# Decode attention over a long key/value cache: loads with 24 KB rows, fewer places, another order and cut of the last loads, and the even head turned at once

## The chip, the cores and the metric

One core of a Trainium2 chip runs the whole program; nothing else runs beside it. The metric is device time in microseconds (us) of one execution, as the median of several. The median of the kernel before moves by 0.3 us between rounds (2007.43 to 2007.76).

## The reference

```python
# x: 1x1x640;  k_cache, v_cache: 32 heads x 32768 keys x 192, bf16;  wq: 640x6144;  wo: 6144x640
h  = x + attention(layernorm(x), k_cache, v_cache, wq, wo)     # one query, softmax over 32768 keys a head
h2 = h + relu(layernorm(h) @ w1) @ w2                          # w1: 640x1536, w2: 1536x640
```

One token attends over a cache of 2 x 403 MB. Nearly all the bytes are read once and used in a few operations, so moving them is the first suspect for the bound; the profile below agrees (DMA queue 98.3%, busiest compute engine 74%).

## The kernel before

Keys and values come in loads of 32 keys per partition: 128 partitions x 12,288 bytes, 1.5 MB, in five places (buffers) for keys and five for values. Of each 32 keys, TensorE turns (transposes) and multiplies 20 (`jp`), VectorE multiplies and sums 12. The product with V follows one chunk later.

```python
J = 32
for h in range(H):
    parts = [(J, 20)] * NC                       # (keys per partition, of these on TensorE)
    if h == H - 1:
        parts = [(J, 20)] * (NC - 1) + [(16, 10), (8, 4), (8, 4)]
...
kpool = ctx.enter_context(tc.tile_pool(name="kpool", bufs=5))
vpool = ctx.enter_context(tc.tile_pool(name="vpool", bufs=5))
...
def load_kv(g):
    h, c, k0, jc, jp = chunks[g]
    kt = kpool.tile([P, J * Dh], bf16, tag="kt", name="kt")
    nc.sync.dma_start(out=kt[:, 0:jc * Dh],
                      in_=k_hd[h, k0:k0 + P * jc, :].rearrange("(p j) d -> p (j d)", p=P))
    vt = ...                                     # the same for values
...
def load_w(name, src, pool, tag, c0, c1):        # w1 and w2 in half loads, each on 128 partitions
    ...
    nc.sync.dma_start(out=v, in_=src.rearrange("(c p) n -> p c n", p=P)[:, c0:c1, :])
...
def o_turn(pr):                                  # two heads' outputs (192 each) into three columns of 128
    ...                                          # ten f32 products with selection matrices
    nc.scalar.copy(out=oT[:], in_=ps[:])
...
for g in range(G):
    if g == G - 3:
        load_w("w1", ...); load_w("w1", ...); load_w("w2", ...); load_w("w2", ...)
    if g > 0:
        load_kv(g)
    transposes(g)
    if g > 0:
        pv(g - 1)
    scores_pe(g)
    sc = scores_dve(g)
    ...
```

The softmax here doesn't subtract the row's maximum and nothing guards it: scores larger than these inputs give would overflow.

## Time and profile before

| | before |
|---|---|
| time, median (range) | 2007.57 us (2007.49 to 2007.66), three runs |
| span in the profile | 2005.7 us |
| busiest compute engine | PE, 74% |
| DMA queue of the loads | 98.3% of the 16 DMA engines' time |
| rate, mean over the span | 413 GB/s |
| rate in undisturbed stretches | 419 to 425 GB/s |

How to read it: a share of the span near 100% names a suspect, and the chain that ended last tells whether the time hangs on it. Here both say DMA (98.3% of the engines' time, 93% of the chain). The 40 slices of the DMA rate then show where it is less than full, and the finer stretches show why. In a stretch, a packet counts where it starts, so a share can come out a little over 1. The lines are in the prediction and are not repeated, but for the rate in 40 slices, which is not there:

```profile
GB/s 396 423 422 422 423 422 423 420 423 424 421 424 417 423 423 422 424 405 424 423 422 423 395 425 422 423 424 396 423 422 424 423 401 424 422 424 422 423 418 171
```

Two things used throughout are in the trace but not in the printed views: the record of every DMA packet (size, start, duration) and the landing records (one count per DMA engine and load). "Step" below is the time from one packet's start to the next packet's start on the same DMA engine. The **trailing half** are eight DMA engines that count in later (16.5 to 18.7 us after a load's first count near 860 us); that they are the ones that also fetch the program's instructions is inferred from the sizes of the gap and of the fetches. The **leading half** are the other eight. Which physical DMA engines these are, the records do not say; the halves are told apart by the gap between their counts.

### The profile page before, as it was taken

How to read it: one execution, taken by the hardware profiler on the slowest of the kernel's cores; microseconds unless marked ns; L12 is line 12 of the kernel's file. 1: busy time of each engine (PE TensorE's matmuls, PEld its weight loads, DVE VectorE, ACT ScalarE, POOL GpSimd, SP SyncE). 2: the span in 40 equal slices, each digit the busy share in tenths (PEclk: the TensorE clock that was granted, in tenths of full speed). 3: DMA queues.
4: the chain of work that ended last, by engine and by line, in shares of the span. 5: the costliest groups of instructions: out<-in, count | busy, mean ns of one | idle time of the engine just before them, and what ended most of it. 6: DMA issues, size and time to landing. Idle time of an engine off the chain costs nothing.

```text
span 2005.7 us, 62124 instructions
## 1 busy us (share of the span) xinstructions
PE 1485.8 (74%) x28712; PEld 1452.7 (72%) x28712; DVE 1333.4 (66%) x646; ACT 1066.1 (53%) x2206; POOL 0.7 (0%) x6
## 2 busy tenths in 40 slices
PE   5777787867778778776777777877777777777775
PEld 5776686767777668676777776877777777777775
DVE  5766676667676667666766676666676667666664
ACT  4555555555555555555555455554555545555553
POOL 0000000000000000000000000000000000000000
PEclk7665656566665666666565665565565755665656
DMA  9999999999999999999999999999999999999994
GB/s 396 423 422 422 423 422 423 420 423 424 421 424 417 423 423 422 424 405 424 423 422 423 395 425 422 423 424 396 423 422 424 423 401 424 422 424 422 423 418 171
DMA packets 88472, 828.97 MB, mean 413 GB/s; under 512 B 8724, under 2 KB 21524, under 8 KB 22932
## 3 DMA queue, kind: packets, MB, share of 16 engines
q1 hardware_dynamic: 88212, 825.00, 98.3%
q8 instruction: 224, 3.67, 0.7%
q14 instruction: 36, 0.29, 0.0%
HBM read 824.97 MB, written 0.00 MB: 411 GB/s over the span
## 4 chain that ended last, share of the span: by engine, by line
DMA 93%; PE 5%; DVE 1%; SPq 1%; issue 0%; ACT 0%; DVEq 0%; ACTq 0%
DMA kt<-in_A_k_cache_dram 78%; DMA vt<-in_A_v_cache_dram 15%; PE tp L230 3%; DVE pr L257 1%; PE oT_ps L320 1%; PE o_ps L288 0%; SPq L113 0%; PE o_ps L290 0%; PE o_ps L286 0%; DVE sc L260 0%; PE sp L240 0%; SPq L110 0%; PE sp L244 0%; PE sp L242 0%; PE yps L391 0%
## 5 line engine op out<-in xcount | busy, mean ns | idle before, releaser
L231 ACT COPY kT<-tp 128x1024 bf16<-128x1024 bf16 (+1 forms) x1024 | 908.0, 974 | 670.0 <-PE tp L230 670.0
L230 PE MATMUL tp<-ident_b,kt 128*128 128x128 bf16 x7677 | 857.0, 311 | 506.1 <-DMA kt<-in_A_k_cache_dram 506.1
L230 PEld LDWEIGHTS <-kt 128*128 128x128 bf16 x7677 | 794.3, 147 | 534.8 <-DMA kt<-in_A_k_cache_dram 534.8
L257 DVE TENSOR_TENSOR pr<-kt,qb 128x2304 f32<-128x2304 bf16 (+1 forms) x258 | 655.6, 2541 | 613.0 <-DMA kt<-in_A_k_cache_dram 613.0
L260 DVE TENSOR_REDUCE sc<-pr 128x12 f32<-128x2304 f32 (+1 forms) x258 | 654.3, 2536 | 26.5
L286 PEld LDWEIGHTS <-vt 128*128 128x128 bf16 x4096 | 343.4, 104 | 0.0
L288 PEld LDWEIGHTS <-vt 128*128 128x128 bf16 x4096 | 336.6, 104 | 0.0
L290 PEld LDWEIGHTS <-vt 128*128 128x128 bf16 x4096 | 326.8, 101 | 0.0
L286 PE MATMUL o_ps<-pB,vt 128*128 128x1 bf16 x2559 | 233.3, 168 | 0.0
L288 PE MATMUL o_ps<-pB,vt 128*128 128x2 bf16 x2559 | 223.8, 166 | 0.0
L290 PE MATMUL o_ps<-pB,vt 128*128 128x1 bf16 x2559 | 223.3, 164 | 0.0
L240 PE MATMUL sp<-qm,kT 128*128 128x2 bf16 x2559 | 221.8, 164 | 1.5 <-ACT kT L231 1.5
L242 PE MATMUL sp<-qm,kT 128*128 128x1 bf16 x2559 | 221.7, 164 | 0.0
L244 PE MATMUL sp<-qm,kT 128*128 128x1 bf16 x2559 | 221.7, 164 | 0.0
L240 PEld LDWEIGHTS <-kT 128*128 128x128 bf16 x2559 | 205.1, 100 | 1.9 <-ACT kT L231 1.9
L242 PEld LDWEIGHTS <-kT 128*128 128x128 bf16 x2559 | 205.2, 100 | 0.0
L244 PEld LDWEIGHTS <-kT 128*128 128x128 bf16 x2559 | 205.1, 100 | 0.0
L247 ACT ACTIVATE pB<-sp 128x20 bf16<-128x20 f32 (+1 forms) x258 | 48.2, 187 | 184.8 <-PE sp L244 184.8
L288 PE MATMUL o_ps<-pA,vt 128*128 128x2 bf16 x1537 | 142.3, 165 | 0.0
L286 PE MATMUL o_ps<-pA,vt 128*128 128x1 bf16 x1537 | 142.0, 164 | 0.0
L290 PE MATMUL o_ps<-pA,vt 128*128 128x1 bf16 x1537 | 142.0, 164 | 0.0
L267 ACT ACTIVATE pA<-sc 128x12 bf16<-128x12 f32 (+1 forms) x258 | 53.3, 207 | 0.0
(84 smaller groups left out, 452.3 us busy)
## 6 DMA issues: line engine op xcount, KB each, us to landing
kt<-in_A_k_cache_dram SPq DMA_DIRECT2D x255, 1536.0 KB, 29.4
vt<-in_A_v_cache_dram SPq DMA_DIRECT2D x255, 1536.0 KB, 28.6
wq<-in_A_wq_dram SPq DMA_DIRECT2D x8, 960.0 KB, 26.1
wo<-in_A_wo_dram SPq DMA_DIRECT2D x16, 480.0 KB, 27.2
kt<-in_B_w_dram SPq DMA_DIRECT2D x1, 1152.0 KB, 28.6
kt<-in_B_w_dram SPq DMA_DIRECT2D x1, 960.0 KB
vt<-in_B_w_dram SPq DMA_DIRECT2D x1, 960.0 KB, 23.8
vt<-in_B_w_dram SPq DMA_DIRECT2D x1, 768.0 KB
```

Source lines behind the costliest of these rows:

```text
L230: nc.tensor.transpose(out=tp[:, b, :], in_=kt[:, off:off + P], identity=ident_b[:])
L231: nc.scalar.copy(out=kT[:, b0:b0 + nb, :], in_=tp[:, 0:nb, :])
L240: nc.tensor.matmul(sp[:, 2 * i:2 * i + 2], lhsT=kT[:, 3 * i + 1, :], rhs=qm[:, 1:3], start=True, stop=False, skip_group_check=True)
L242: nc.tensor.matmul(sp[:, 2 * i:2 * i + 1], lhsT=kT[:, 3 * i, :], rhs=qm[:, 0:1], start=False, stop=False, skip_group_check=True)
L244: nc.tensor.matmul(sp[:, 2 * i + 1:2 * i + 2], lhsT=kT[:, 3 * i + 2, :], rhs=qm[:, 3:4], start=False, stop=True, skip_group_check=True)
L247: nc.scalar.activation(out=pB[:, 0:JP], in_=sp[:, 0:JP], func=F.Exp, scale=SCALE, accum_out=dsums[:, h, 2 * c + 1:2 * c + 2])
L257: nc.vector.tensor_tensor(out=pr[:, 0:JD, :], in0=kt[:, 0:JD * Dh].rearrange("p (j d) -> p j d", d=Dh), in1=qb[:].unsqueeze(1).to_broadcas ...
L260: nc.vector.reduce_sum(out=sc[:, 0:JD], in_=pr[:, 0:JD, :], axis=mybir.AxisListType.X)
L267: nc.scalar.activation(out=pA[:, 0:JD], in_=sc[:, 0:JD], func=F.Exp, scale=SCALE, accum_out=dsums[:, h, 2 * c:2 * c + 1])
L286: nc.tensor.matmul(o[:, 0:1], lhsT=v[:, 0:P], rhs=p[:, 0:1], start=first, stop=False, skip_group_check=True)
L288: nc.tensor.matmul(o[:, 1:3], lhsT=v[:, P:2 * P], rhs=p, start=False, stop=False, skip_group_check=True)
L290: nc.tensor.matmul(o[:, 3:4], lhsT=v[:, 2 * P:3 * P], rhs=p[:, 1:2], start=False, stop=last, skip_group_check=True)
```

## The change

Its intent is to spend less on each packet, and to shorten the end:

1. Loads of 64 keys per partition, 24 KB rows, in 3 + 3 places; compute still goes in chunks of 32.
2. The last loads: w1 and w2 first, then all remaining keys, then all remaining values. w2 is cut by partitions so that some DMA engines carry less of it.
3. The even head's output columns are turned as soon as that head is done, so that behind the last head only four products remain.

```diff
+    JL = 64
     J = 32
...
+    full = [(JL, [(J, 20), (J, 20)])] * (Sk // (P * JL))
+    ends = full[:-1] + [(40, [(20, 12), (20, 12)]), (16, [(16, 10)]), (8, [(8, 4)])]
+    NEND = 3
...
-    kpool = ctx.enter_context(tc.tile_pool(name="kpool", bufs=5))
-    vpool = ctx.enter_context(tc.tile_pool(name="vpool", bufs=5))
+    kpool = ctx.enter_context(tc.tile_pool(name="kpool", bufs=3))
+    vpool = ctx.enter_context(tc.tile_pool(name="vpool", bufs=3))
...
+    def load_part(ld, src, pool, tag, name):
+        h, k0, jl = loads[ld]
...
+        t = pool.tile([P, size], bf16, tag=tag, name=name)
+        nc.sync.dma_start(out=t[:, 0:jl * Dh], in_=src[h, k0:k0 + P * jl, :].rearrange("(p j) d -> p (j d)", p=P))
+        return t
...
-    def load_w(name, src, pool, tag, c0, c1):
+    def load_w(name, src, pool, tag, rows):
...
+        for r0, r1 in rows:
+            nc.sync.dma_start(out=v[r0:r1], in_=src.rearrange("(c p) n -> p c n", p=P)[r0:r1])
...
+            if not odd:
+                ps = mm_bank([P, 2], f32, "oT_ps")
+                parts = [(0, 1, "all", 0), (0, 1, "u_l", 2), (0, 1, "l_u", 3), (1, 2, "l_l", 1), (1, 2, "u_l", 3)]
+                oT_t[pr] = small.tile([P, 3], bf16, tag="oT", name="oT")
+            else:
+                ps = mm_bank([P, 2], f32, "oT_ps")
+                parts = [(0, 2, "l_u", 0), (0, 1, "u_u", 2), (1, 2, "all", 3), (1, 2, "u_l", 0)]
...
+            if end == 0 and c0 == 0:
+
+                load_w("w1", B_w1, kpool, "kt", [(0, P)])
+                load_w("w2", B_w2, vpool, "vt", [(0, 112), (112, 120), (120, 124), (124, 126), (126, 128)])
+                for i in range(NEND):
+                    load_k(ld + i)
+                for i in range(NEND):
+                    load_v(ld + i)
```

More of the change, by code (lines that the diff above doesn't have):

```diff
@@ L40 @@
     FT = Dff // P
+    JL = 64
     J = 32
     QG = 4
-    assert Sk % (P * J) == 0 and 2 * Dh == 3 * P and H % QG == 0 and H % 2 == 0
-    NC = Sk // (P * J)
+    assert Sk % (P * JL) == 0 and 2 * Dh == 3 * P and H % QG == 0 and H % 2 == 0
+    full = [(JL, [(J, 20), (J, 20)])] * (Sk // (P * JL))
+    ends = full[:-1] + [(40, [(20, 12), (20, 12)]), (16, [(16, 10)]), (8, [(8, 4)])]
+    NEND = 3
+    loads = []
     chunks = []
     for h in range(H):
-        parts = [(J, 20)] * NC
-        if h == H - 1:
-            parts = [(J, 20)] * (NC - 1) + [(16, 10), (8, 4), (8, 4)]
-        k0 = 0
-        for c, (jc, jp) in enumerate(parts):
-            chunks.append((h, c, k0, jc, jp))
-            k0 += P * jc
+        k0 = c = 0
+        for jl, parts in (ends if h == H - 1 else full):
+            off = 0
+            for jc, jp in parts:
+                chunks.append((h, c, len(loads), off, jc, jp))
+                off += jc
+                c += 1
+            assert off == jl
+            loads.append((h, k0, jl))
+            k0 += P * jl
         assert k0 == Sk
@@ L59 @@
     NCM = max(NCH)
-    NBM = max(q[4] for q in chunks) * Dh // P
-    JDM = max(q[3] - q[4] for q in chunks)
+    NBM = max(q[5] for q in chunks) * Dh // P
+    JDM = max(q[4] - q[5] for q in chunks)
     const = ctx.enter_context(tc.tile_pool(name="const", bufs=1))
-    kpool = ctx.enter_context(tc.tile_pool(name="kpool", bufs=5))
-    vpool = ctx.enter_context(tc.tile_pool(name="vpool", bufs=5))
+    kpool = ctx.enter_context(tc.tile_pool(name="kpool", bufs=3))
+    vpool = ctx.enter_context(tc.tile_pool(name="vpool", bufs=3))
     wqp = ctx.enter_context(tc.tile_pool(name="wqp", bufs=2))
@@ L97, in load_wq @@
     def load_wq(gq):
-        t = wqp.tile([P, DT, QG * Dh], bf16, name="wq")
-        nc.sync.dma_start(out=t[:], in_=wq_view[:, :, gq * QG * Dh:(gq + 1) * QG * Dh])
+        t = wqp.tile([P, DT * QG * Dh], bf16, tag="wq", name="wq")
+        t = t[:].rearrange("p (c n) -> p c n", c=DT)
+        nc.sync.dma_start(out=t, in_=wq_view[:, :, gq * QG * Dh:(gq + 1) * QG * Dh])
         wq_t[gq] = t
@@ L105, in load_wo, with load_k, load_v @@
         wo_t[pr] = t
-    def load_kv(g):
-        h, c, k0, jc, jp = chunks[g]
-        kt = kpool.tile([P, J * Dh], bf16, tag="kt", name="kt")
-        nc.sync.dma_start(out=kt[:, 0:jc * Dh],
-                          in_=k_hd[h, k0:k0 + P * jc, :].rearrange("(p j) d -> p (j d)", p=P))
-        vt = vpool.tile([P, J * Dh], bf16, tag="vt", name="vt")
-        nc.sync.dma_start(out=vt[:, 0:jc * Dh],
-                          in_=v_hd[h, k0:k0 + P * jc, :].rearrange("(p j) d -> p (j d)", p=P))
-        kt_t[g], vt_t[g] = kt, vt
-    w_t = {}
-    def load_w(name, src, pool, tag, c0, c1):
-        t = pool.tile([P, J * Dh], bf16, tag=tag, name=tag)
-        n = src.shape[1]
-        v = t[:, 0:(c1 - c0) * n].rearrange("p (c n) -> p c n", n=n)
-        nc.sync.dma_start(out=v, in_=src.rearrange("(c p) n -> p c n", p=P)[:, c0:c1, :])
-        for c in range(c0, c1):
-            w_t[name, c] = v[:, c - c0, :]
+    def load_part(ld, src, pool, tag, name):
+        h, k0, jl = loads[ld]
+        if ld == len(loads) - 1:
+            pool, tag, size = wqp, "wq", DT * QG * Dh
+        else:
+            size = JL * Dh
+        t = pool.tile([P, size], bf16, tag=tag, name=name)
+        nc.sync.dma_start(out=t[:, 0:jl * Dh], in_=src[h, k0:k0 + P * jl, :].rearrange("(p j) d -> p (j d)", p=P))
+        return t
+    def load_k(ld):
+        kt_t[ld] = load_part(ld, k_hd, kpool, "kt", "kt")
+    def load_v(ld):
+        vt_t[ld] = load_part(ld, v_hd, vpool, "vt", "vt")
+    w_t = {}
+    def load_w(name, src, pool, tag, rows):
+        n, N = src.shape[0] // P, src.shape[1]
+        assert n * N <= JL * Dh
+        t = pool.tile([P, JL * Dh], bf16, tag=tag, name=tag)
+        v = t[:, 0:n * N].rearrange("p (c n) -> p c n", n=N)
+        for r0, r1 in rows:
+            nc.sync.dma_start(out=v[r0:r1], in_=src.rearrange("(c p) n -> p c n", p=P)[r0:r1])
+        for c in range(n):
+            w_t[name, c] = v[:, c, :]
     load_wq(0)
@@ L155 @@
     nc.vector.memset(dsums[:], 0.0)
-    o_part = [const.tile([P, 4], f32, name=f"o_part{i}") for i in range(4)]
+    o_part = [const.tile([P, 4], f32, name=f"o_part{i}") for i in range(2)]
+    o_even = [const.tile([P, 2], f32, name=f"o_even{i}") for i in range(2)]
+    for t in o_even:
+        nc.vector.memset(t[:], 0.0)
     attT = aps.tile([P, DT], f32, name="attT")
@@ L220, in transposes @@
         def transposes(g):
-            kt = kt_t[g]
-            h, c, k0, jc, jp = chunks[g]
+            h, c, ld, c0, jc, jp = chunks[g]
+            kt = kt_t[ld]
             NB = jp * Dh // P
@@ L228, in transposes @@
                 for b in range(nb):
-                    off = (jc - jp) * Dh + (b0 + b) * P
+                    off = (c0 + jc - jp) * Dh + (b0 + b) * P
                     nc.tensor.transpose(out=tp[:, b, :], in_=kt[:, off:off + P], identity=ident_b[:])
@@ L235, in scores_pe @@
             kT = kT_t.pop(g)
-            h, c, k0, jc, JP = chunks[g]
+            h, c, ld, c0, jc, JP = chunks[g]
             qm = qm_t[h]
@@ L251, in scores_dve @@
         def scores_dve(g):
-            kt = kt_t.pop(g)
-            h, c, k0, jc, jp = chunks[g]
+            h, c, ld, c0, jc, jp = chunks[g]
+            kt = kt_t[ld]
             JD = jc - jp
@@ L256, in scores_dve @@
             pr = prp.tile([P, JDM, Dh], f32, name="pr")
-            nc.vector.tensor_tensor(out=pr[:, 0:JD, :], in0=kt[:, 0:JD * Dh].rearrange("p (j d) -> p j d", d=Dh),
+            nc.vector.tensor_tensor(out=pr[:, 0:JD, :], in0=kt[:, c0 * Dh:(c0 + JD) * Dh].rearrange("p (j d) -> p j d", d=Dh),
                                     in1=qb[:].unsqueeze(1).to_broadcast([P, JD, Dh]), op=A.mult)
@@ L263, in exp_dve @@
         def exp_dve(g, sc):
-            h, c, k0, jc, jp = chunks[g]
+            h, c, ld, c0, jc, jp = chunks[g]
             JD = jc - jp
@@ L271, in pv @@
         def pv(g):
-            h, c, k0, jc, jp = chunks[g]
+            h, c, ld, c0, jc, jp = chunks[g]
             JD = jc - jp
-            vt, pA, pB = vt_t.pop(g), pA_t.pop(g), pB_t.pop(g)
+            vt, pA, pB = vt_t[ld], pA_t.pop(g), pB_t.pop(g)
             if c == 0:
@@ L284, in pv @@
                 last = c == NCH[h] - 1 and i == len(order) - 1
-                v = vt[:, j * Dh:(j + 2) * Dh]
+                v = vt[:, (c0 + j) * Dh:(c0 + j + 2) * Dh]
                 nc.tensor.matmul(o[:, 0:1], lhsT=v[:, 0:P], rhs=p[:, 0:1],
@@ L308, in o_scale, with o_turn @@
             s = den_t.pop(h)
-            nc.vector.tensor_scalar_mul(out=o_part[h % 4][:], in0=o_t.pop(h)[:], scalar1=s[:, 1:2])
+            nc.vector.tensor_scalar_mul(out=o_part[h % 2][:], in0=o_t.pop(h)[:], scalar1=s[:, 1:2])
         oT_t = {}
-        def o_turn(pr):
-            e, o = o_part[2 * pr % 4], o_part[(2 * pr + 1) % 4]
-            ps = mm_bank([P, 3], f32, "oT_ps")
-            parts = [(0, "all", e, 0), (0, "u_l", e, 2), (0, "l_u", e, 3),
-                     (1, "l_l", e, 1), (1, "u_l", e, 3), (1, "l_u", o, 0), (1, "u_u", o, 2),
-                     (2, "all", o, 3), (2, "u_l", o, 0), (2, "l_u", o, 1)]
-            for i, (b, w, src, r) in enumerate(parts):
-                nc.tensor.matmul(ps[:, b:b + 1], lhsT=sel[w][:], rhs=src[:, r:r + 1], start=(i == 0), stop=(i == len(parts) - 1),
-                                 skip_group_check=True)
-            oT = small.tile([P, 3], bf16, tag="oT", name="oT")
-            nc.scalar.copy(out=oT[:], in_=ps[:])
-            oT_t[pr] = oT
+        def o_turn(h):
+            pr, odd = divmod(h, 2)
+            o = o_part[h % 2]
+            if not odd:
+                ps = mm_bank([P, 2], f32, "oT_ps")
+                parts = [(0, 1, "all", 0), (0, 1, "u_l", 2), (0, 1, "l_u", 3), (1, 2, "l_l", 1), (1, 2, "u_l", 3)]
+                oT_t[pr] = small.tile([P, 3], bf16, tag="oT", name="oT")
+            else:
+                ps = mm_bank([P, 2], f32, "oT_ps")
+                parts = [(0, 2, "l_u", 0), (0, 1, "u_u", 2), (1, 2, "all", 3), (1, 2, "u_l", 0)]
+            for i, (b0, b1, w, r) in enumerate(parts):
+                nc.tensor.matmul(ps[:, b0:b1], lhsT=sel[w][:], rhs=o[:, r:r + b1 - b0], start=(i == 0),
+                                 stop=(i == len(parts) - 1), skip_group_check=True)
+            if not odd:
+                nc.vector.tensor_copy(out=oT_t[pr][:, 0:1], in_=ps[:, 0:1])
+                nc.vector.tensor_copy(out=o_even[pr % 2][:, 0:1], in_=ps[:, 1:2])
+            else:
+                nc.vector.tensor_add(out=oT_t[pr][:, 1:3], in0=ps[:], in1=o_even[pr % 2][:])
         def project(pr):
@@ L332, in project @@
                                      stop=(pr == H // 2 - 1 and b == 2 and n == DT - 1), skip_group_check=True)
-        load_kv(0)
+        load_k(0)
+        load_v(0)
         q_rows(0)
@@ L337 @@
         for g in range(G):
-            h, c, k0, jc, jp = chunks[g]
-            if g == G - 3:
-                half = (DT + 1) // 2
-                load_w("w1", B_w1, kpool, "kt", 0, half)
-                load_w("w1", B_w1, vpool, "vt", half, DT)
-                load_w("w2", B_w2, kpool, "kt", 0, FT // 2)
-                load_w("w2", B_w2, vpool, "vt", FT // 2, FT)
-            if g > 0:
-                load_kv(g)
+            h, c, ld, c0, jc, jp = chunks[g]
+            end = ld - (len(loads) - NEND)
+            if end == 0 and c0 == 0:
[5 more added lines that the diff above has]
+                    load_v(ld + i)
+            elif end < 0 and c0 == 0 and g > 0:
+                load_k(ld)
+                load_v(ld)
             if c == 1 and h % 2 == 0:
@@ L360 @@
                 o_scale(h - 1)
-            if c == 1 and h > 0 and h % 2 == 0:
-                o_turn(h // 2 - 1)
+            if c == 1 and h > 0:
+                o_turn(h - 1)
             if c == 2 and h > 0 and h % 2 == 0:
@@ L373 @@
         o_scale(H - 1)
-        o_turn(H // 2 - 1)
+        o_turn(H - 1)
         project(H // 2 - 1)
```

## The prediction

> **What bounds the kernel now.** I read the page from the top: the busy shares, the 40 slices, the DMA queues, the chain that ended last, the DMA issues. Then I read the stretches, the sync queue's waits and, below the printed views, the trace's records of single DMA packets and of landings.
>
> ```profile
> PE 1485.8 (74%) x28712; PEld 1452.7 (72%) x28712; DVE 1333.4 (66%) x646; ACT 1066.1 (53%) x2206; POOL 0.7 (0%) x6
> ...
> DMA  9999999999999999999999999999999999999994
> ...
> q1 hardware_dynamic: 88212, 825.00, 98.3%
> q8 instruction: 224, 3.67, 0.7%
> ...
> DMA 93%; PE 5%; DVE 1%; SPq 1%; issue 0%; ACT 0%; DVEq 0%; ACTq 0%
> ...
> kt<-in_A_k_cache_dram SPq DMA_DIRECT2D x255, 1536.0 KB, 29.4
> vt<-in_A_v_cache_dram SPq DMA_DIRECT2D x255, 1536.0 KB, 28.6
> ```
>
> No compute engine is above 74%. The DMA row is full until the last slice, and 93% of the chain is DMA. So the time is the time in which the DMA engines move 825 MB, plus a start and an end. The keys and values come in 510 loads of 1.5 MB, each with one 12,288-byte packet for each of 128 partitions; a load lands 29 us after its issue, so about eight are under way.
>
> ```profile
> core 0: us, PE busy (x) PEld busy (x) DVE busy (x) ACT busy (x) POOL busy (x), PEclk, DMA share, GB/s
> 860.00:880.00 20.00, 13.64 (x304) 13.37 (x302) 13.27 (x9) 10.64 (x23) 0.00 (x0) 0.65 1.01 419
> 880.00:900.00 20.00, 17.05 (x279) 16.89 (x280) 13.12 (x7) 9.98 (x19) 0.00 (x0) 0.61 0.95 379
> 900.00:920.00 20.00, 14.41 (x309) 13.79 (x307) 12.58 (x5) 10.49 (x23) 0.00 (x0) 0.54 1.01 425
> 1940.00:1955.00 15.00, 11.10 (x221) 10.93 (x220) 10.45 (x5) 8.26 (x18) 0.00 (x0) 0.50 1.00 406
> 1955.00:1970.00 15.00, 10.93 (x229) 10.75 (x228) 10.56 (x5) 8.37 (x18) 0.00 (x0) 0.74 0.56 229
> 1970.00:1988.00 18.00, 7.22 (x195) 7.05 (x192) 7.26 (x6) 5.13 (x17) 0.00 (x0) 0.59 0.82 296
> ```
>
> In these stretches the last two columns are the DMA share and rate. It holds 419 to 425 GB/s, dips around 880 us (also near 1130, 1370 and 1630 us) and falls to about half at 1955 us. These dips look like time to win, but the landing records say otherwise. Each load's completion is counted once per DMA engine, 16 times. For a load near 860 us eight engines report within 5 us of each other and the other eight 16.5 to 18.7 us later; near 1970 us the gap is 19 to 22 us. So **eight engines run behind and eight ahead**, and a dip is the eight leaders running out of issued work. What separates them is instruction fetching: 224 packets of 16 KB, each of which stops the data of one engine for 1.05 to 1.1 us, and nearly every 12 KB packet after one takes about 0.5 us longer (some 960 ns where 460 are usual). 224 / 8 = 28 fetches x 1.55 us = 43 us for each laggard; the leaders' lead of 22 us at the end plus about 20 us in the dips (steps back of 5 us or so) is the same sum. The laggards have no such idle time: from the first packet at 1.7 us to the last landing at 1988.1 us they are fed. **The laggards' list of packets is the time.**
>
> [...] the mean step from one packet's start to the next on its engine (outliers left out) is 53.0 ns for 1280 B, 62.4 for 1536, 119.0 for 3072, 234.1 for 6144 and 460.1 for 12,288. Between the first and last the slope is (460.1 - 53.0) / 11,008 = 0.0370 ns per byte, and the intercept 53.0 - 47.3 = **5.7 ns a packet**. The line fits the sizes between within 1.2 ns. [...] 16 / 0.0370 = 433 in this trace, and 422 are reached: little can be won. [...]
>
> **The change part by part.** *Rows of 24 KB.* For each engine, key and value packets fall from 510 x 8 + 6 x 8 = 4128 to 254 x 8 + 6 x 8 = 2080. The bytes are the same, so what goes is 2048 intercepts: 2048 x 5.7 = 11.7 us. [...] (the fastest steps are 456 ns, the mean 460.1); if that goes by packet rather than by byte, a removed packet is worth up to 8.3 ns, and if the fastest steps alone count, 4.7. I take 6.0: **-12.3 us** (-9.6 to -17). One completion write of 5.9 ns per engine and load goes too, for about 255 loads: **-1.5 us**.
>
> *Places 5 + 5 to 3 + 3.* They hold more, 6 x 3 MB against 10 x 1.5. A key place is free once VectorE has done both halves, 2 x (2.54 + 2.54) = 10.2 us after landing. The laggards reach the next load for that place 5 loads later, 5 x 7.4 = 37 us. A value place is free after the next keys' first transposes and one product with V, about 7.4 + 3.4 + 1.3 = 12 us after landing, against 37 again. Some 25 us of margin: the laggards never starve. Leaders can lead by about 20 us as before, which costs nothing. **0 us.** TensorE needs 5.8 us for 32 keys (1486 / 258) and the transfers give it 7.4.
>
> *The last loads.* w1 and w2 go ahead of the last keys, and w2 is cut by partitions so that 16 of them skip half of the engines: an engine so relieved has 84 packets instead of 96, 12 x 53 ns = **-0.6 us**, if those are the laggards. Keys before values lets scores run under the values' transfer, but the chunks of 20 keys that stand behind the first value load then follow each other on TensorE. By the rates of the old end (113 ns a transpose, 0.026 us a small product) I get some 4.3 us from the last landing to the last head's scaling; before it is 1991.1 - 1988.1 = 3.0. **+1.3 us.**
>
> *The even head turned at once.* The chain's end has this:
>
> ```profile
> 1991.08 4.41 PE oT_ps L320 x20
> 1995.52 0.17 ACT oT L323
> 1995.73 0.55 PE attT L330 x15
> ```
>
> Twenty records are ten f32 products in two passes, all exposed. After the change four remain behind the last head: 4.41 x 4/10 = 1.76, **-2.65 us**. The rest is moved under transfers, where the added 50 VectorE instructions cost nothing (66% busy). PE has 16 fewer products, ACT 15 fewer copies. The closing copy becomes an addition of about the same 0.17 us.
>
> *Fetches.* The program shrinks by a few hundred of its 62,124 instructions, so again 28 per laggard. The 0.5 us lost by the packet after a fetch is not plainly tied to packet size: where 1536-byte packets followed, four in a row took 158 to 179 ns instead of 65, 0.42 us in all, like a slow half microsecond. If it were one lost packet time it would double at 24 KB: 28 x 0.46 = 13 us. I allow **+2 us**.
>
> Sum: -12.3 - 1.5 - 0.6 + 1.3 - 2.65 + 2 = -13.8 us, so 2007.6 - 13.8 = **1994 us**, 0.7% faster.
>
> **The rivals.** (a) *A fetch costs a longer packet.* For it: the lost 0.5 us is close to one 12 KB packet's 460 ns. Against: the small packets after a fetch. It would leave some 2005 us. (b) *Long rows are cut in two in the queue.* Then 12 KB packets stay and only the completion writes and the end are won: about 2004 us. For it: no row above 16 KB occurs in this trace. Against: the 12 KB rows pass whole. (c) *Places take the place of the old waits.* The sync queue already waits 165.7 us for the products with V before a value load:
>
> ```profile
> SPq L113 <- DMA vt<-in_A_v_cache_dram: 591.6, 176, 4.9
> SPq L110 <- DMA kt<-in_A_k_cache_dram: 472.2, 182, 4.9
> SPq L113 <- PE o_ps L290: 165.7, 168, 9.2
> ```
>
> Today most of its waiting is for earlier loads to land (eight under way); after the change it will be mostly for PE and DVE, and a throttled TensorE (granted 0.5 in some stretches, up to 18.9 of 20 us busy) could delay issues. It must eat 25 us before a laggard starves. If it did, each hole would cost a few us: 2005 to 2030. (d) *The half-rate stretch at the end is won back* as well as the dips: 15 us at half rate would be 7 us, and the four dips some 10 more, giving about 1977. Against: the laggards ran through all of it. (e) *Jitter goes by packet*: 1988.
>
> **Range and chances.** The small-term sums give 1994. Rival (e) and a free fetch pull to 1987; (a) and (b) push to 2005, each with perhaps one chance in eight. So 8 in 10 lie in 1985 to 2002. A gain of 2% means below 1967, faster than the 433 GB/s line allows with the fetches in: 0.02. A loss of 2%, above 2048, needs a starving queue: 0.01. Within 2%: 0.97.
>
> **What would show each step.** Packets of 24,576 B, half as many as before, with a step of about 912 to 915 ns: the main term. Steps of 920, or packets of 12,288, refute it. The first packet after a fetch near 1.4 us (0.5 lost) rather than 1.85 (0.94 lost) decides rival (a). Landings should still split eight and eight. The steady stretches should show about 425 GB/s. The sync queue should wait for PE and DVE rather than for landings, with no stretch where all engines drop. The turn in the end chain should have 8 records and some 1.8 us. I am wrong if the mean rate falls, if a load waits so long that the laggards idle, or if the time moves by more than 25 us, since no term of the sum is that large.

The 5.7 ns a packet comes from the steps measured in the trace of the kernel before, and the "jitter" of rival (e) is the difference there between the mean step (460.1 ns) and the fastest (456 ns).

## The result

The changed kernel takes **2000.83 us** (2000.26 to 2001.32, four runs) against 2007.54 us before (2007.49 to 2007.66, four runs). A ratio in this document is the mean time of one kernel's fast runs over that of the other's of the same rounds, so not quite the ratio of the medians. Here it is 0.9966 (95% interval 0.9949 to 0.9984): within 2%, 6.7 us faster by the medians. That lies inside the stated range (1985 to 2002), but the gain is half of the 13.6 us that was predicted.

The profile page of the changed kernel, the lines that answer to those of before: busy shares, the rate in 40 slices, the DMA queues, the chain's shares, and the two large groups of issues with their size and time to landing.

```profile
PE 1384.8 (69%) x28680; PEld 1346.9 (67%) x28680; DVE 1336.7 (67%) x696; ACT 1067.5 (53%) x2191; POOL 0.7 (0%) x6
...
GB/s 402 427 426 425 427 426 428 425 427 427 428 428 422 427 426 428 427 418 427 427 425 424 412 427 427 427 422 410 428 426 425 417 415 428 425 426 420 422 321 159
...
q1 hardware_dynamic: 51332, 824.99, 98.0%
q8 instruction: 224, 3.67, 0.7%
...
DMA 82%; PE 14%; DVE 3%; ACT 1%; issue 0%; SPq 0%; DVEq 0%; ACTq 0%
...
kt<-in_A_k_cache_dram SPq DMA_DIRECT2D x127, 3072.0 KB, 37.1
vt<-in_A_v_cache_dram SPq DMA_DIRECT2D x127, 3072.0 KB, 33.3
```

The same bytes go in 51,332 packets instead of 88,212, so a 24 KB row is one packet (32,512 records of 24,576 bytes). The usual slice now has 425 to 428 GB/s instead of 422 to 424. The fetches are 224 as before. The second last slice has 321 GB/s, where before it had 418. So the body became faster and the end became slower.

The sync queue's waits changed their nature, as expected. It waits for engines to give places back, not for earlier loads to land (columns: who waited for whom, us in total, times, longest):

```profile
SPq L123 <- PE o_ps L310: 1326.4, 124, 14.0
SPq L123 <- DVE pr L277: 386.9, 124, 14.9
```

This costs nothing: a load still lands 33 to 37 us after its issue, so the DMA engines have work queued, and the landing records show the first and the last DMA engine of a load 19 to 24 us apart from 850 us on (5 us at 190 us), much as before. The end of the chain is as planned too, eight records in 1.88 us where twenty took 4.41:

```profile
1987.07 1.88 PE oT_ps L345 x8
1988.97 0.17 DVE oT L351
1989.19 0.42 PE attT L357 x10
```

The stretches at the end of the changed kernel (last two columns: DMA share and GB/s) show the loss:

```profile
1910.00:1925.00 15.00, 10.86 (x208) 10.77 (x206) 9.86 (x9) 7.00 (x16) 0.00 (x0) 0.61 1.00 421
1925.00:1940.00 15.00, 6.43 (x193) 6.05 (x191) 7.67 (x3) 6.63 (x15) 0.00 (x0) 0.73 0.85 218
1940.00:1955.00 15.00, 10.76 (x216) 10.68 (x216) 10.22 (x4) 8.03 (x16) 0.00 (x0) 0.50 0.67 181
1955.00:1970.00 15.00, 0.00 (x0) 0.00 (x0) 0.00 (x0) 0.00 (x0) 0.00 (x0) 0.50 1.02 247
```

Before, a stretch at half rate had a DMA share of about a half (1955 to 1970 us: 0.56, 229 GB/s): the leading half was idle, and the trailing half ran at its own full pace (its 12,288-byte packets took the usual 460 ns in the median). Here 1925 to 1940 us has a share of 0.85 and still only 218 GB/s, and 1955 to 1970 us has all DMA engines busy (1.02) at 247 GB/s. **Busy and slow is a different illness from idle.** The packet records of these stretches say what it is. From 1928 to 1938 us the leading half writes the 112-partition piece of w2: its 1280-byte packets take 117 to 121 ns (55 usual), and beside them the trailing half's 24,576-byte packets take 1,640 to 1,800 ns in the median up to 1936 us (912 usual). From 1950 to 1966 us it is the other way round: the trailing half writes w1 and w2, the leading half the last keys beside the small pieces of w2, and 15,360-byte packets take about 1,000 to 1,800 ns in the median (573 usual).

For the trailing half, whose list of packets is the time, this makes, from its landings:

- one load while the leaders write w2: 1930.4 to 1941.2 us, 10.8 instead of 7.3 us, and 0.8 us in the load before it: 4.3 us;
- w1: 1948.5 to 1957.9 us, 9.4 us where 40 packets of 3072 bytes at 119 ns are 4.8: 4.6 us;
- its own part of w2: to 1966.7 us, 8.8 us where 84 packets of 1280 bytes at 53 ns are 4.5: 4.3 us.

That is 13.2 us, and the suspect is the cut of w2 by partitions. The rest of the document tests this and the other terms.

### The profile page after: what moved, and what is told of

It reads as the page before. It is cut to its first block, busy times and chain, and to the rows that moved or that the text cites. A ratio compares the mean times of both kernels' runs of the same rounds, so it can differ in the third digit from the quotient of the medians.

```text
span 1999.2 us, 61496 instructions
## 1 busy us (share of the span) xinstructions
PE 1384.8 (69%) x28680; PEld 1346.9 (67%) x28680; DVE 1336.7 (67%) x696; ACT 1067.5 (53%) x2191; POOL 0.7 (0%) x6
## 3 DMA queue, kind: packets, MB, share of 16 engines
q1 hardware_dynamic: 51332, 824.99, 98.0%
## 4 chain that ended last, share of the span: by engine, by line
DMA 82%; PE 14%; DVE 3%; ACT 1%; issue 0%; SPq 0%; DVEq 0%; ACTq 0%
DMA kt<-in_A_k_cache_dram 79%; PE tp L250 10%; DMA vt<-in_B_w_dram 2%; DVE pr L277 2%; PE o_ps L308 1%; PE o_ps L310 1%; PE o_ps L306 1%; DVE sc L280 1%; DMA vt<-in_A_v_cache_dram 1%; ACT kT L251 1%; PE sp L264 0%; PE sp L260 0%; PE qps L216 0%; PE sp L262 0%; PE den L317 0%
## 5 line engine op out<-in xcount | busy, mean ns | idle before, releaser
L250 PE MATMUL tp<-ident_b,kt 128*128 128x128 bf16 x7677 | 777.4, 290 | 573.4 <-DMA kt<-in_A_k_cache_dram 558.6
L250 PEld LDWEIGHTS <-kt 128*128 128x128 bf16 x7677 | 718.8, 137 | 598.4 <-DMA kt<-in_A_k_cache_dram 569.5
L306 PEld LDWEIGHTS <-vt 128*128 128x128 bf16 x4096 | 334.9, 101 | 10.8 <-DMA vt<-in_A_v_cache_dram 8.1
L308 PEld LDWEIGHTS <-vt 128*128 128x128 bf16 x4096 | 329.3, 101 | 0.0
L310 PEld LDWEIGHTS <-vt 128*128 128x128 bf16 x4096 | 322.2, 99 | 1.1 <-issue 1.1
L260 PE MATMUL sp<-qm,kT 128*128 128x2 bf16 x2559 | 225.5, 164 | 13.2 <-ACT kT L251 9.6
L306 PE MATMUL o_ps<-pB,vt 128*128 128x1 bf16 x2559 | 228.1, 167 | 5.6 <-DMA vt<-in_A_v_cache_dram 5.1
L264 PE MATMUL sp<-qm,kT 128*128 128x1 bf16 x2559 | 224.9, 164 | 2.8 <-issue 1.3
L262 PE MATMUL sp<-qm,kT 128*128 128x1 bf16 x2559 | 224.9, 164 | 2.1 <-issue 2.1
L310 PE MATMUL o_ps<-pB,vt 128*128 128x1 bf16 x2559 | 220.7, 164 | 0.7 <-issue 0.5
```

The source lines that it names most:

```text
L250: nc.tensor.transpose(out=tp[:, b, :], in_=kt[:, off:off + P], identity=ident_b[:])
L260: nc.tensor.matmul(sp[:, 2 * i:2 * i + 2], lhsT=kT[:, 3 * i + 1, :], rhs=qm[:, 1:3], start=True, stop=False, skip_group_check=True)
L262: nc.tensor.matmul(sp[:, 2 * i:2 * i + 1], lhsT=kT[:, 3 * i, :], rhs=qm[:, 0:1], start=False, stop=False, skip_group_check=True)
L264: nc.tensor.matmul(sp[:, 2 * i + 1:2 * i + 2], lhsT=kT[:, 3 * i + 2, :], rhs=qm[:, 3:4], start=False, stop=True, skip_group_check=True)
L306: nc.tensor.matmul(o[:, 0:1], lhsT=v[:, 0:P], rhs=p[:, 0:1], start=first, stop=False, skip_group_check=True)
L308: nc.tensor.matmul(o[:, 1:3], lhsT=v[:, P:2 * P], rhs=p, start=False, stop=False, skip_group_check=True)
```

## The experiments

Eleven kernels were run. The first theory: the 24 KB rows bring more than predicted, and the cut of w2 loses most of it. The rivals: w2's short rows or the place of the weights ahead of the last keys cause the stall; more loads cause it; or the gain of the rows is smaller, and the end is as good as it gets.

### e1_w2_whole: w2 in one load

```diff
-                load_w("w2", B_w2, vpool, "vt", [(0, 112), (112, 120), (120, 124), (124, 126), (126, 128)])
+                load_w("w2", B_w2, vpool, "vt", [(0, P)])
```

> The changed kernel with one edit: w2 comes in one load of 128 partitions instead of five loads cut at partitions 112, 120, 124 and 126. Theory (the cut stalls everything): in the changed kernel's trace, while the 112-partition piece of w2 runs on the leading or on the trailing half of the DMA engines, all packets take about twice as long (24,576 B: 1,700 ns against 912; 1,280 B: 115 against 52); the trailing half loses about 4.3 us while the leaders write w2, 4.6 us in w1 and 4.3 us in its own w2, some 13 us in all. Without the cut: 2000.8 - 13 + 0.6 (12 more packets) = about 1988 us, and no 24,576-byte packet above 1,300 ns except after a fetch. Rival (w2's short rows of 1,280 B, or w1 and w2 standing ahead of the last keys, make the stall whatever the cut): 2000 to 2001 us.

Measured: **1988.93 us** (1988.24 to 1989.09), ratio to before 0.9906 (0.9892 to 0.9921). One edit gives 11.9 us. The stretches of the same times:

```profile
1925.00:1940.00 15.00, 9.70 (x222) 9.38 (x221) 10.49 (x6) 8.52 (x17) 0.00 (x0) 0.73 0.75 296
1940.00:1955.00 15.00, 6.59 (x193) 6.14 (x190) 7.65 (x3) 6.54 (x15) 0.00 (x0) 0.73 0.80 303
1955.00:1970.00 15.00, 8.77 (x169) 8.51 (x170) 9.93 (x7) 5.91 (x15) 0.00 (x0) 0.50 0.71 284
```

Share and rate go together again (0.75 x 425 = 319, against 296 with short packets among them): what is busy runs near full pace. While w2 is written the 1280-byte packets take 55 to 59 ns in the median and the large ones 912 to 931. The theory holds; w2's short rows and the order of weights and keys are unchanged here, so they are not the cause by themselves.

### e2_w2_five_blocks: five loads, cut another way

```diff
-                load_w("w2", B_w2, vpool, "vt", [(0, 112), (112, 120), (120, 124), (124, 126), (126, 128)])
+                load_w("w2", B_w2, vpool, "vt", [(0, 3), (3, 6), (6, 8), (8, 10), (10, 12)], by_block=True)
...
+            if by_block:                       # in load_w: row blocks, on all 128 partitions
+                nc.sync.dma_start(out=v[:, r0:r1, :], in_=s[:, r0:r1, :])
```

> As the changed kernel, but w2's five loads are cut over its twelve row blocks (3, 3, 2, 2, 2), each on all 128 partitions. Theory (cut by partitions is the cause): as with one load, 1987 to 1990 us, packets at their usual length. Rival (five loads instead of one, more issues and completions, are the cause): near 2000 us.

Measured: 1988.11 us (1988.04 to 1988.40), ratio 0.9903 (0.9888 to 0.9918). Five loads are no worse than one as long as each covers the 128 partitions. So it is not the number of loads; it is the cut by partitions.

### e3_w2_112_16: only one cut

```diff
-                load_w("w2", B_w2, vpool, "vt", [(0, 112), (112, 120), (120, 124), (124, 126), (126, 128)])
+                load_w("w2", B_w2, vpool, "vt", [(0, 112), (112, 128)])
```

> As the changed kernel, but w2 is cut only once, in 112 and 16 partitions. Theory (the 112-partition piece, seven partitions to a DMA engine, is what stalls): about as slow as the changed kernel, 1997 to 2002 us, with 24,576-byte packets near 1,700 ns while the leaders write it. Rival (the four small pieces on 8, 4, 2 and 2 DMA engines stall): about 1990 us.

Measured: 1999.80 us (1998.87 to 2000.28), ratio 0.9961 (0.9946 to 0.9975). Without the small pieces it is nearly as slow as the changed kernel (2000.83), and while the leading half writes the 112-partition piece the 24,576-byte packets beside it take about 1,740 ns. The 112-partition piece is enough; the small pieces on few DMA engines aren't needed for the loss.

### e4_before_w2_cut: the cut in the old kernel

```diff
-        nc.sync.dma_start(out=v, in_=src.rearrange("(c p) n -> p c n", p=P)[:, c0:c1, :])
+        rows = [(0, 112), (112, 120), (120, 124), (124, 126), (126, 128)] if name == "w2" else [(0, P)]
+        for r0, r1 in rows:
+            nc.sync.dma_start(out=v[r0:r1], in_=src.rearrange("(c p) n -> p c n", p=P)[r0:r1, c0:c1, :])
```

> The kernel before with one edit: both half loads of w2 are cut at partitions 112, 120, 124 and 126. Theory (cut by partitions): slower than before by 8 to 15 us, 2016 to 2022 us, with packets at twice their length in the last 50 us. Rival (the loss needs the changed kernel's places or its order of last loads): within 3 us of before, 2005 to 2010 us.

Measured: 2014.09 us (2013.99 to 2014.58), ratio 1.0033 (1.0016 to 1.0050): 6.5 us slower than before (2007.55 in these rounds). The sign is the theory's and the size is below its range. From 1954 to 1957 us, while w2 is written, packets of 1280 bytes take 102 to 113 ns and the 12,288-byte ones beside them 787 to 896 ns, in the median of each microsecond (460 usual): the slowing is about as strong as in the changed kernel. Why it costs only half as much was not tested.

### e8_keys_cut_112: the cut with other data

This one keeps w2 whole and cuts a key load, whose rows are long and lie in one piece.

```diff
+        cut = name == "kt" and k0 == 0 and h in (8, 16, 24)
+        for r0, r1 in ([(0, 112), (112, P)] if cut else [(0, P)]):
+            nc.sync.dma_start(out=t[r0:r1, 0:jl * Dh], in_=s[r0:r1])
```

> The changed kernel with w2 in one load, and one key load in each of three heads (8, 16, 24) cut at partition 112 (112 and 16 partitions, rows of 24 KB). Theory [...]: in each of the three places the 112-partition piece, 7 packets an engine, and whatever runs beside it on the other half take about 1,700 ns instead of 912 a packet: 7 x 0.8 = 5.5 us lost by the trailing half in its own turn and about as much in the leaders' turn, so 11 us each and 20 to 35 us in all. Rival (w2's short source rows are needed for the stall): within 2 us of w2 in one load.

Measured: 2051.79 us (2046.77 to 2053.82), ratio 1.0211 (1.0196 to 1.0227). That is 62.9 us more than w2 in one load, 21 us for each cut load, twice what was expected. The stretches around the first of the three:

```profile
460.00:480.00 20.00, 16.13 (x323) 15.53 (x322) 15.47 (x7) 12.01 (x24) 0.00 (x0) 0.59 1.00 425
480.00:500.00 20.00, 13.20 (x243) 13.09 (x242) 11.38 (x5) 10.26 (x24) 0.00 (x0) 0.50 1.02 243
500.00:520.00 20.00, 3.09 (x86) 2.74 (x84) 2.60 (x2) 2.62 (x7) 0.00 (x0) 0.59 1.03 220
```

All DMA engines are busy (1.02, 1.03) at about half the rate, from 484 to 523 us, first while the leading half writes the cut load and then while the trailing half does. I had counted only the seven packets of the large piece, at 1,700 ns. Here most medians lie between 1,800 and 2,100 ns, and e9_cuts_at_start shows that the piece of 16 partitions is slow as well; how the loss divides between the two was not worked out. The interval of the ratio spans 2%, so whether the kernel is slower by 2% is unclear; that the cuts cost tens of microseconds is not. The rival (w2's rows) is out: the cut stalls long rows that lie in one piece, too.

### e9_cuts_at_start: how long a packet takes by the number of partitions

```diff
+        cuts = {1: [0, 64, P], 3: [0, 112, P], 5: list(range(0, P + 1, 16))}.get(ld, [0, P]) if name == "kt" else [0, P]
+        for r0, r1 in zip(cuts, cuts[1:]):
+            nc.sync.dma_start(out=t[r0:r1, 0:jl * Dh], in_=s[r0:r1])
```

> One look at packet lengths. The changed kernel with w2 in one load, and three key loads near the start, where all 16 DMA engines are still within a few us of each other, cut by partitions: the second in 64 + 64, the fourth in 112 + 16, the sixth in eight pieces of 16. [...] Rival (any cut by partitions halves the rate[...]): 1,800 ns in all of them.

Measured in one look: most 24,576-byte packets take 1,900 to 1,930 ns while the two pieces of 64 are written, some 1,430 to 1,630 ns in the 112 piece, 2,400 to 3,400 ns in the 16 piece behind it, and 2,650 to 2,870 ns in the eight pieces of 16. The stretches with no cut, with 64 + 64, with no cut, and with 8 x 16:

```profile
10.00:20.00 10.00, 5.79 (x75) 5.63 (x76) 6.18 (x3) 5.21 (x10) 0.00 (x0) 1.00 1.00 428
22.00:34.00 12.00, 1.89 (x74) 1.80 (x71) 2.07 (x1) 2.00 (x6) 0.00 (x0) 0.67 0.94 196
42.00:52.00 10.00, 6.33 (x190) 6.03 (x188) 7.28 (x3) 6.30 (x15) 0.00 (x0) 0.84 1.01 428
97.00:109.00 12.00, 7.38 (x172) 7.12 (x169) 7.20 (x6) 5.01 (x10) 0.00 (x0) 0.50 1.04 149
```

The rival, the same factor for every cut, is out. Against the usual 912 ns the packets are 2.1 times as long in the two pieces of 64 (196 GB/s in their stretch), 1.6 to 1.8 times in the 112 piece, 2.6 to 3.7 times in the 16 piece behind it and about 3.0 times in the eight pieces of 16 (149 GB/s). So the smaller pieces had the longer packets here. The last number is not that of one piece by itself: value packets lie in the same stretch, and several pieces on different partitions were under way at once (their first counts are about 2.8 us apart, the counts of one spread over some 10 us). Why they are longer was not shown: no run sees which DMA engine writes which partition, or what a packet waits for.

### e5_rows_12k: the row size by itself

The places, the order and the end of e1_w2_whole, with each load of 64 keys done as two DMAs of 32 keys into the two halves of its place.

```diff
-        nc.sync.dma_start(out=t[:, 0:jl * Dh], in_=src[h, k0:k0 + P * jl, :].rearrange("(p j) d -> p (j d)", p=P))
+        step = J if jl == JL else jl
+        for j0 in range(0, jl, step):
+            a = k0 + P * j0
+            nc.sync.dma_start(out=t[:, j0 * Dh:(j0 + step) * Dh],
+                              in_=src[h, a:a + P * step, :].rearrange("(p j) d -> p (j d)", p=P))
```

> The changed kernel with w2 in one load, and each load of 64 keys per partition cut into two DMAs of 32 keys (12 KB rows) into the two halves of the same place. Places, order of use and the end are the same; only packet size and number of DMAs go back. Theory (row size is a gain of its own): 254 x 8 packets more per DMA engine at 920.3 - 911.8 = 8.5 ns a pair (measured steps, 12,288 B against 24,576 B) is 17.3 us, plus 254 completions at 5.9 ns = 1.5 us: 18 to 19 us slower than the kernel with w2 in one load, about 2006 to 2007 us if that has 1988. Rival (by intercept 5.7 ns a packet, as predicted): 13 us slower. Rival (the gain is from places or order): within 3 us of it.

Measured: 2007.87 us (2007.12 to 2008.18), ratio to before 1.0000 (0.9987 to 1.0014). Against e1_w2_whole that is **18.9 us** for the row size and the number of DMAs. The steps explain it: 460.15 ns for 12,288 bytes in this kernel, 911.9 ns for 24,576 in e1_w2_whole. 2 x 460.15 - 911.9 = 8.4 ns a removed packet, x 254 x 8 = 17.1 us, and 254 completions x 5.9 ns = 1.5 us: 18.6 us. The rival of 13 us (5.7 ns a packet) is out.

### e6_before_turn: the turn by itself

```diff
-            if c == 1 and h > 0 and h % 2 == 0:
-                o_turn(h // 2 - 1)
+            if c == 1 and h > 0:
+                o_turn(h - 1)                  # with o_turn, o_part and o_even of the changed kernel
```

> The kernel before with only the turn changed: the even head's output columns turned one head earlier, four products left behind the last head. Theory: -2.6 us (the turn in the end chain 4.41 us before, 1.88 us in the changed kernel, ACT copy and DVE addition alike), 2004.9 us. Rival (hidden or given back by the added VectorE work and banks): 2007 us or more.

Measured: 2005.49 us (2005.15 to 2006.18) against 2007.76 in its rounds, ratio 0.9989 (0.9977 to 1.0002): 2.3 us by the medians. The interval just reaches no change, but the end chain has the turn at 1.88 us where it was 4.41, so the size is as expected.

### e7_last_interleaved: keys and values in turn at the end

```diff
                 for i in range(NEND):
                     load_k(ld + i)
-                for i in range(NEND):
                     load_v(ld + i)
```

> The changed kernel with w2 in one load and the last six loads in the order keys, values, keys, values. Theory of keys first (its intent): the end from last landing to the last head's scaling becomes longer, because the last keys' turns, scores and exponentials come after the last transfers: +1 to +3 us against w2 in one load. My own working in the prediction, that keys first makes the end 1.3 us longer, would give -1 us here.

Measured: 1987.08 us (1987.00 to 1987.44), ratio 0.9898 (0.9884 to 0.9911): 1.85 us faster than e1_w2_whole. Keys first is a loss; the two intervals of the ratio overlap, so this rests on the ranges of the times, which don't, and on the traces. The last packet of the loads starts at 1969.75 us with keys first and at 1969.25 us in turn, so the transfers end nearly together; the turn of the last head begins 5.8 us after that in the one and 4.2 us after it in the other. With keys first, the products with V that stand before the last chunks on TensorE wait for the first value load: the chain of waits of e1_w2_whole goes through that load, issued at 1948.80 us and landed at 1966.97, into the product with V, where the chain of e7_last_interleaved goes from a key load into the turns.

### e10_pe16 and e11_pe24: is the trailing half's list really the time?

If the trailing DMA engines set the time, their instruction fetches are in it, and a shorter program is faster though no wait of TensorE is in the chain. Both kernels start from e7_last_interleaved and change only how many of each 32 keys go to TensorE.

```diff
-    full = [(JL, [(J, 20), (J, 20)])] * (Sk // (P * JL))
+    full = [(JL, [(J, 16), (J, 16)])] * (Sk // (P * JL))      # e11_pe24: 24
```

> The fastest version so far (w2 in one load, last loads keys and values in turn; 1987.1 us) with 16 instead of 20 of each 32 keys on TensorE and 16 on VectorE. Same bytes; TensorE has 50,731 instead of 56,827 instructions, so some 24 fewer instruction fetches of 256 instructions each, three fewer for each trailing DMA engine. Theory (the trailing engines' list, fetches at about 1.55 us each in it, is the time): 3 x 1.55 = 4.7 us faster, about 1982.4 us, although no wait on TensorE is taken away. Rival (bytes alone bound it): 1987 us. Second rival (VectorE, 16 keys at 0.42 us = 6.8 us of the 7.3 us that a chunk's transfers take, becomes the bound): 1995 us or more.

(The 256 instructions to a fetch are in the page of the changed kernel: 28,680 each for PE and PEld, 57,360 together, and 224 fetches.)

> The same in the other direction: 24 of each 32 keys on TensorE, 62,923 instructions, 24 more fetches. Theory of the fetches: 4.7 us slower than 1987.1, about 1991.8 us. Rival (bytes alone): 1987 us. If TensorE's own time (about 11% more than 5.4 us a chunk) starts to hold places: over 1995 us.

Measured: e10_pe16 **1982.51 us** (1982.29 to 1982.57), ratio 0.9875 (0.9859 to 0.9892); e11_pe24 1991.56 us (1991.41 to 1992.17), ratio 0.9921 (0.9906 to 0.9935). Their pages, first 16 keys (busy line and fetch queue), then 24 (fetch queue):

```profile
PE 1278.5 (65%) x25632; PEld 1219.6 (62%) x25632; DVE 1737.4 (88%) x696; ACT 897.8 (45%) x1937; POOL 0.7 (0%) x6
...
q8 instruction: 200, 3.28, 0.7%
```

```profile
q8 instruction: 248, 4.06, 0.8%
```

200 and 248 fetches against 224 (with 16 keys 6,096 fewer TensorE instructions, PE and PEld of the pages taken together, and 24 fewer fetches, so 254 to a fetch), and -4.6 and +4.5 us where 3 x 1.55 = 4.7 was expected both ways. If all 16 DMA engines shared the fetches, 24 of them would be 1.5 each, 2.3 us, half of what was measured: so I infer that the fetches lie on half of them. Nor do the data packets get shorter or longer with the work of the compute engines: without the outliers above 967 ns, a 24,576-byte packet takes 915.6 ns on average with 16 keys, 915.3 with 20 and 915.1 with 24. Bytes alone as the bound is out, and no loss from VectorE at 88% shows. e10_pe16 is the fastest version, 24.9 us below before (2007.43 in its rounds).

## Why the prediction was right or wrong

The measured terms nearly add up: rows -18.9, cut of w2 +11.9, turn -2.3, keys first +1.85 make -7.45 us; measured -6.7. (Each term comes from its own pair of kernels, so a microsecond is left to that.) The predicted sum was -13.8, from these steps:

- **"Rows of 24 KB": right mechanism, size too small.** -12.3 and -1.5 us were predicted, 18.9 measured. The mis-sized factor is the 6.0 ns taken for a removed packet, which is 8.4: the jitter in the mean step does go by packet, the case noted as up to 8.3 and as rival (e). The packet records show it: without outliers, the mean length lies above the commonest by 3.5 ns at 12,288 bytes (463.5 against 460) and by 3.3 ns at 24,576 (915.3 against 912), not by twice as much. Where this spread comes from, no run shows. Rival (b), rows cut in two in the queue, is refuted by the packet size.
- **"The last loads": the step that failed.** It read the cut of w2 as work taken from some DMA engines, -0.6 us. The runs show a cut by partitions that slows the packets then under way, on both halves, for +11.9 us net. The prediction took packet lengths from loads on 128 partitions and used them for one on 112; no load of w2's size in the old trace is on fewer than 128 partitions, and the case was not listed among the rivals. Why such a cut stalls stays open. It also doubted "if those are the laggards", rightly: of the eight DMA engines that write the 8-partition piece six counted in by 1954 us and two 12 us later, so they are of both halves.
- **Keys before values**: +1.3 us predicted, +1.85 measured. Right, against the change's intent.
- **"Places 5 + 5 to 3 + 3": right.** e5_rows_12k has the new places with old rows and is as fast as before, where the other two small terms (-2.3 and +1.85) nearly cancel. Rival (c), places as a new bound, is out, although the waits did change sides.
- **"The even head turned at once": right**, -2.65 predicted, -2.3 measured, and the turn itself 1.88 us where 1.76 was worked out.
- **"Fetches": +2 us was allowed, nothing was found.** A fetch takes 1.07 us in the median, before and after, and stops its DMA engine's data for that time: in both traces, behind 215 of the 224 fetches, a lengthened packet starts about 14 ns before the fetch ends. The packet after a fetch takes 1,407 ns in the median (912 usual), 951 before (460 usual): 495 and 491 ns lost. The loss is about half a microsecond at both packet sizes, and rival (a) is out.
- **Rival (d), the dips won back: rightly left aside.** They are the leaders' idle time. That the trailing half's list is the time was only argued in the prediction; e10_pe16 and e11_pe24 have since shown it.

So the total fell into the range by luck, because two errors partly cancelled: the rows gave about 5 us more than predicted and the cut took 12 us more. Without the cut the kernel has 1988.9 us, below the predicted value by 5.

## What to carry to other kernels

When a kernel is bound by DMA, find which DMA engines finish last and count their packets, completions and instruction fetches: here that list was the time, and packets of 24 KB (18.9 us) or a shorter program (4.6 us for 24 fetches) shortened it, while the idle time of the others (the dips, and the stretch at 229 GB/s at the old end) is in none of the terms that add up to the measured gain. Write loads on all 128 partitions. If one must be cut, cut it so that every piece is on all 128: w2 in five such pieces was no slower than in one (1988.11 against 1988.93 us). Don't cut it by partitions to balance a microsecond: it cost 11.9 us for w2 and 21 us for a key load, and every such cut tried here made most packets under way about 1.6 times as long or more, in other loads beside it too (1,640 to 1,800 ns instead of 912). In a profile tell idle from slow: here a low rate with a low DMA share (229 GB/s at 0.56) was missing work, with packets of the usual 460 ns; a low rate with a full share (247 GB/s at 1.02) meant that each packet took longer (about 1,000 to 1,800 ns instead of 573).
